# Giving the decoding of w_out its own tiles and a later turn, and re-running the order search of a fused attention and gated-MLP kernel

## The chip, the cores and the metric

One core of a Trainium2 chip runs the whole program. The metric is the device time of one execution in microseconds (us). The kernel before takes 417.23 us (median of 3 runs, 416.99 to 417.38). PE is the matmul engine, PEld its weight loads, DVE the vector engine, ACT the scalar engine, POOL the GpSimd engine, and SP the engine that issues every DMA here.

## The reference

The inputs are four batches of 768 positions with 8 heads of 64. Everything is in f32 except that some weights come as f64, which the kernel must decode itself.

```
scores = (q @ k^T) / 8;  keep key j for query i if j < 4 or 0 <= i - j < 128
a      = softmax(scores over the kept keys);   x = a @ v           (heads side by side: 512 columns)
h      = relu(x @ w_in)  (512 -> 1024);        u, v = halves of h
vn     = (v - mean(v)) / sqrt(var(v) + 1e-6)   (over the 512 columns)
vs     = w_spatial @ vn + b_spatial            (mixes the 768 positions of a batch)
out    = (u * vs) @ w_out                      (512 -> 512)
```

## The kernel before

Positions are cut into tiles of 128, so a batch has six. A tile's attention is done in two halves of four heads; the 48 halves of the four batches are numbered 0 to 47. The program speaks of *pieces*, each a few instructions of one engine:

- **Attention.** SP loads `qkraw` and `vraw`. PE makes scores (`sc`), DVE adds the mask and finds the row's extreme (`pexp` and `nm`, L1022), ACT takes the exponential (L1027). The weights are split into a high and a low f16 part (`p`; a helper's lines, L698 or L707 for the high part, L714 for the low). SP turns both with DMA transposes (`pT`), PE multiplies with the values (`av`), DVE divides (`x`, L1132 to L1134). The same split and transposing give `xT`.
- **MLP.** PE makes `ps_v` and `ps_u` from `xT` and w_in. ACT applies the relu (`vr`, `u`), DVE and POOL normalise `vr` and split it into `vn`. When all six tiles of a batch have their `vn`, PE makes the twelve *spatial products* `ps_s` of that batch. DVE gates them (`g`, L1243, then L1247 on DVE or POOL), they are split into `g2`, and PE makes the six *output products* `ps_o`. ACT copies them out (`ob`), SP stores them.
- **Precision.** Nearly every product is three f16 matmuls (high by high, high by low, low by high). Twelve matmuls make one piece `ps_v`, `ps_u` or `ps_o`, 18 make one `ps_s`.
- **Decoding.** w_in (eight chunks of 128 by 512) and w_out (four chunks) come as f64 bit patterns. Each chunk is loaded by SP (`dec`, 512 KB), goes through two steps of ACT (L793 into `w32`, L795 into `wtmp`), three of DVE (L791, L798, L800, on `w32`), an add on POOL (L803), a high part on ACT (L700) and a low part on DVE (L721). Listings show `w32` as `w`, often with a number.
- **Checks.** Maxima of all tables are gathered. At the very end of the program PE, DVE and PE again turn them into one flag (`allmax`, `ps_row`, `ps_col`, `marks`, `found`, L762 to L898). All engines read the flag and branch.

**What sets the order.** Nothing is scheduled by the hardware beyond each engine's own queue, which runs in program order. A planner in the kernel (`Plan`) sorts the pieces by rank (the table `WHEN`, in units of one attention half), derives what must follow what, and then plays all pieces through a model of the engines; whoever may start first in that model goes next, and may also choose the engine of a piece that has several (`ENGINES`). `order()` then repeats: it plays the result backwards to get every piece's distance to the end, shakes these distances by a random amount per kind or per piece, and plays forward again. The list `PASSES` holds the seeds, the sizes of the shaking and the numbers of repetitions. Its last result is the program.

Tiles come from rings of places. `"u"` (seven places), for one, is shared by `u`, the raw w_spatial rows and `dec`; `"vn"` (twelve) by `vn` and `w32`; `"vr"` (three) by `vr`, `ob` and `wtmp`. In the rings that `IN_TURN` lists, `"u"` and `"vn"` among them, a tile gets its place strictly in the order of the ranks. PSUM for the MLP products is a ring of two banks (`"mm"`), so each product waits until the product before the last has been read out by ACT or DVE.

Of the kernel before, what the change touches and what calls it, by code (L numbers as in the profile page):

```python
# [70 lines left out]
def general_path(tc, wf, qk, v, w_in, w_sp, b_sp, w_out, out):  # L71
# [164 lines left out]
UB, VNB, G2B, XTB, P16B, PTB, QKB, QPB, PEB, VB, VRB = 7, 12, 12, 2, 2, 2, 2, 2, 2, 3, 6  # L236
GB = 2

WHEN = {
# [3 lines left out]
    "u gap": 1.24, "u relu": 0.2, "s": 2.69, "s gap": 0.68, "s rest": 0.0, "gate": 0.0, "g split": 0.41, "o": 0.2,  # L243
    "o gap": 0.0, "o copy": 0.36, "o store": 0.44, "w_in 1": -5.48, "w_in 0": -0.25, "w_sp": 5.67, "w_out": 3.53,
    "w_in 1 gap": 0.0, "w_in 0 gap": 0.75, "w_sp gap": 0.24, "w_out gap": 1.39,
}
# [79 lines left out]
class Plan:  # L326
# [183 lines left out]
    def order(self):  # L510

        self.prepare()
        kinds, kind = {}, {}
        for p in self.pieces:
            name, which = ((p[6] or p[5])[0])[:2]
            key = name, str(which[0] if isinstance(which, tuple) else which), p[2] if isinstance(p[2], str) else ""
            kind[p[1]] = kinds.setdefault(key, len(kinds))
        self.end = self.settle([p[0] for p in self.ps])
        for seed, of_kind, of_piece, passes in PASSES:
            for k in range(passes):  # L520
                prio = self.backward()
                if k == 0:
                    prio = [x + of_kind / 100.0 * scatter(seed, kind[p[1]]) + of_piece / 100.0 * scatter(seed + 7936, 100000 + p[1])
                            for x, p in zip(prio, self.ps)]
# [68 lines left out]
def fast_path(tc, st, scalars, qk, v, v0, vs, w_in, w_sp, w_rows, b_sp, b_col, w_out, out):  # L593
# [7 lines left out]
    with (  # L601
# [40 lines left out]
        def next_p16(name):  # L642
# [6 lines left out]
            "w32": ("vn", sb([P, 512], F32, "vn", VNB)), "vn": ("vn", sb([P, 2, DM], F16, "vn", VNB)),  # L649
            "wtmp": ("vr", sb([P, 512], I32, "vr", VB)), "vr": ("vr", sb([P, DM], F32, "vr", VB)),  # L650
            "ob": ("vr", sb([P, DM], F32, "vr", VB)),
# [18 lines left out]
                 "p16": P16B, "pT": PTB, "x": 1, "x16": 2, "xT": XTB, "g": GB, "g2": G2B,  # L670
                 "sc": BANKS["sc"], "av": BANKS["av"], "mm": BANKS["mm"], "ksink": 1}
        rings.update({f"{kind}{j}": 1 for kind in ("kslot", "vslot", "vsink") for j in range(4)})
# [110 lines left out]
        def decode(rank, src, i, c, f0):  # L783

            words = lambda: tl("dec", i).rearrange("p (n two) -> p n two", two=2)
            lo, hi = lambda: words()[:, :, 0], lambda: words()[:, :, 1]
            w = lambda: tl("w32", i)
# [17 lines left out]

# [39 lines left out]
        def w_out_all():  # L845
            r0, gap = WHEN["w_out"], WHEN["w_out gap"]
            for c in range(KC):
                i = ("out", 0, c)
                decode(r0 + gap * c, w_out, i, c, 0)
                high(r0 + gap * c, "w_in high", 512, lambda c=c, i=i: (wout[:, 0, c, :], tl("w32", i)),  # L850
                     [("w32", i)], [("wout", c, 0)], OUT_SCALE)
                low_scaled(r0 + gap * c, 512, lambda c=c, i=i: (wout[:, 1, c, :], tl("w32", i), wout[:, 0, c, :]), OUT_SCALE,
                           [("w32", i), ("wout", c, 0)], [("wout", c, 1)])
# [98 lines left out]
        def whole(b):  # L952
            return b < WHOLE
# [35 lines left out]
        def scores(i, b, t, hf, h2, r, n):  # L989
# [35 lines left out]
            def exped(q):  # L1025
# [3 lines left out]
            keys = [(f"kslot{kslot(b, x)}", (b, x)) for x in ((t, t - 1, 5) if t == 4 else (t, t - 1) if t else (t,))]  # L1029
            plan.add(r, "PE", (0.06 + n / 4 * (1.04 if t else 0.56)) if whole(b) else 0.03 + n / 2 * (0.336 if t else 0.18), product,  # L1030
                     ([("qkraw", (b, t)), ("k0room", 0)] if whole(b) else [("qp", (b, t))]) + keys, banks,
# [176 lines left out]
        def u_half(b, c0, d, r):  # L1208
# [3 lines left out]
            def product(e):  # L1212
# [8 lines left out]
            k = first["u"] + (b * NT // 2 + c0) * KC + d  # L1221
            plan.add(r + WHEN["u relu"], "a", 0.55, lambda e: nc.scalar.activation(  # L1222
                tl("u", (b, c0))[:, d, :], tl("ps_u", i)[:, :TC], AF.Relu, scale=G_SCALE / (V_SCALE * IN_SCALE),
# [155 lines left out]
```

## Time and profile before

| | us |
|---|---|
| median of 3 runs (416.99 to 417.38) | 417.23 |
| the profiled execution, its own time | 416.92 |
| its span, first to last instruction | 415.1 |
| PE busy (share of the span) | 389.8 (94%) |
| DVE busy | 325.7 (78%) |
| ACT busy | 299.3 (72%) |
| POOL busy | 164.9 (40%) |
| chain that ended last: PE / DVE / ACT | 63% / 26% / 4% |

A busy share is a mean over the whole span, and this program has two halves that differ, so the share of each stretch is read and not the mean. The chain that ended last is followed back from the last instruction: each piece in it is what released the next one.

### The profile page before, as it was taken

Reading aid. Unit: us, or ns where it says so; the run is one execution under the profiler, and the core shown is the slowest. Engines: PE = TensorE matmul, PEld = TensorE weight load, DVE = VectorE, ACT = ScalarE, POOL = GpSimd, SP = SyncE. Lnnn points to the kernel's source line nnn. Section 1 sums busy time; section 2 is a strip of 40 time slices with the busy share of each in tenths; the row PEclk is TensorE's granted clock in tenths of the full one; section 3 lists DMA queues with packets and bytes.
Section 4 is the critical chain, followed back from the end, with each engine's and each line's share of the span. In section 5 each row is a group of like instructions: output and inputs, shape, how many; then the busy total and the mean of one; then the engine's idle time right before and its main releaser. Section 6 shows DMA issues by size and latency. Waiting matters only on the chain.

```text
span 415.1 us, 9851 instructions
## 1 busy us (share of the span) xinstructions
PE 389.8 (94%) x3635; PEld 274.7 (66%) x3635; DVE 325.7 (78%) x908; ACT 299.3 (72%) x695; POOL 164.9 (40%) x204
## 2 busy tenths in 40 slices
PE   3899699899999999999999999999999999999992
PEld 2686355667766757667767677577677686688740
DVE  2999999999999989878899797787897855256311
ACT  4987989888897788687867886858567643366740
POOL 4442345763755645324454853233236432100000
PEclk9999998999999999999999999999999999999998
DMA  7999999978478788757968587594783493602011
GB/s 229 386 325 252 267 202 181 222 115 172 108 168 173 187 152 198 182 120 148 221 159 182 81 208 183 130 209 93 148 173 89 86 201 34 204 27 76 37 66 58
DMA packets 137047, 66.93 MB, mean 161 GB/s; under 512 B 118432, under 2 KB 122272, under 8 KB 136992
## 3 DMA queue, kind: packets, MB, share of 16 engines
q1 hardware_dynamic: 136992, 66.24, 70.3%
q8 instruction: 30, 0.49, 0.5%
q14 instruction: 25, 0.20, 0.2%
HBM read 31.09 MB, written 6.29 MB: 90 GB/s over the span
## 4 chain that ended last, share of the span: by engine, by line
PE 63%; DVE 26%; ACT 4%; issue 3%; DMA 3%; SPq 0%; DVEq 0%; ACTq 0%
PE ps_s L732 19%; PE ps_o L732 14%; PE ps_u L732 11%; PE ps_v L732 9%; DVE pexp L1022 5%; DVE p L714 5%; PE sc L1017 5%; ACT pexp L1027 2%; PE av L1112 2%; DMA dec<-w_in 2%; PE av L1113 2%; PE av L1114 2%; DVE vring L721 1%; DVE w L791 1%; DVE wsp L721 1%
## 5 line engine op out<-in xcount | busy, mean ns | idle before, releaser
L1027 ACT ACTIVATE pexp<-pexp,nm 128x260 f32<-128x260 f32 (+1 forms) x192 | 82.9, 484 | 24.9 <-DVE nm L1022 24.5
L732 PE MATMUL ps_s<-wsp,vn 128*128 128x256 f16 x864 | 99.3, 273 | 0.8 <-DVE g L1243 0.4
L732 PEld LDWEIGHTS <-vn 128*128 128x128 f16 x864 | 83.5, 98 | 14.4 <-issue 3.1
L732 PE MATMUL ps_v<-win,xT 128*128 128x512 f16 x288 | 69.1, 391 | 3.6 <-DMA xT<-x 3.2
L732 PE MATMUL ps_u<-xT,win 128*128 128x256 f16 x576 | 69.7, 275 | 2.8 <-ACT vr L1173 1.9
L732 PE MATMUL ps_o<-wout,g 128*128 128x512 f16 x288 | 65.3, 379 | 1.2 <-DVE g L1243 0.4
L732 PEld LDWEIGHTS <-win 128*128 128x128 f16 x576 | 55.2, 98 | 13.9 <-issue 5.3
L714 DVE TENSOR_TENSOR p<-pexp,p 128x16 f16<-128x16 f32 (+2 forms) x65 | 50.0, 783 | 7.5 <-ACT p L698 6.3
L732 PEld LDWEIGHTS <-xT 128*128 128x128 f16 x288 | 27.8, 100 | 36.7 <-issue 5.7
L732 PEld LDWEIGHTS <-g 128*128 128x128 f16 x288 | 27.5, 98 | 32.6 <-issue 2.2
L714 POOL TENSOR_TENSOR x<-x,x 128x512 f16<-128x512 f32 x24 | 30.9, 1290 | 38.3 <-ACT x L698 36.6
L698 ACT CAST p<-pexp 128x1024 f16<-128x1024 f32 (+2 forms) x68 | 40.6, 621 | 1.3 <-DMA pT<-p 0.7
L1243 DVE SCALAR_TENSOR_TENSOR g<-ps_s,b_bc 128x256 f32<-128x256 f32 x48 | 20.2, 422 | 19.1 <-PE ps_s L732 18.6
L1112 PE MATMUL av<-vring,pT 128*128 128x65 f16 x328 | 34.1, 193 | 0.0
L1114 PE MATMUL av<-vring,pT 128*128 128x65 f16 x328 | 34.0, 193 | 0.0
L1113 PE MATMUL av<-vring,pT 128*128 128x65 f16 x328 | 34.0, 193 | 0.0
L1112 PEld LDWEIGHTS <-pT 128*128 128x128 f16 x328 | 30.2, 97 | 1.5 <-issue 0.6
L1189 POOL TENSOR_TENSOR rs<-rs,mhalf 128x1 f32<-128x1 f32 x24 | 16.3, 681 | 36.9 <-DVE rs L1183 31.5
L1113 PEld LDWEIGHTS <-pT 128*128 128x128 f16 x328 | 30.1, 97 | 0.6
L1222 ACT ACTIVATE u<-ps_u 128x256 f32<-128x256 f32 x48 | 18.2, 379 | 16.6 <-PE ps_u L732 16.4
L1114 PEld LDWEIGHTS <-pT 128*128 128x128 f16 x328 | 30.0, 97 | 0.0
L698 ACT CAST g<-g 128x256 f16<-128x256 f32 x36 | 14.5, 403 | 20.4 <-DVE g L1247 18.2
(139 smaller groups left out, 722.4 us busy)
## 6 DMA issues: line engine op xcount, KB each, us to landing
qkraw<-qk_t SPq DMA_DIRECT2D x18, 512.0 KB, 4.4
out<-ob SPq DMA_DIRECT2D x24, 256.0 KB, 2.5
vraw<-v_s SPq DMA_DIRECT2D x22, 256.0 KB, 3.7
dec<-w_in SPq DMA_DIRECT2D x8, 512.0 KB, 8.4
wrow<-w_sp_rows SPq DMA_DIRECT2D x6, 384.0 KB, 4.8
dec<-w_out SPq DMA_DIRECT2D x4, 512.0 KB, 6.5
wsp<-qk_t SPq DMA_DIRECT2D x6, 256.0 KB, 6.7
qkraw<-qk_t SPq DMA_DIRECT2D x6, 256.0 KB, 5.1
```

The source lines that it names most:

```text
L698: nc.scalar.copy(o, x)
L714: eng[e].tensor_tensor(out=o, in0=x, in1=hi, op=ALU.subtract)
L732: nc.tensor.matmul(o, a, m, start=(i == 0), stop=(i == n - 1))
L1017: nc.tensor.matmul(o, qp[rows, qi, hp, :], keys(kring[:, ki], rows), start=(m == 0), stop=(m == 2))
L1022: nc.vector.tensor_tensor_reduce(out=po, in0=o, in1=mask, scale=-0.125 if whole(b) else -0.125 / Q_SCALE ** 2, scalar=3.0e38, op0=ALU.add, ...
L1027: nc.scalar.activation(po, po, AF.Exp, bias=nm()[:, h2 + q:h2 + q + 1], scale=-1.0)
L1112: nc.tensor.matmul(o[:, h], ph, vh, start=(t < 2 and j == 0), stop=False)
L1113: nc.tensor.matmul(o[:, h], ph, vl, start=False, stop=False)
L1114: nc.tensor.matmul(o[:, h], pl, vh, start=False, stop=(j == nb - 1 and (t < 2 or h == HH - 1)))
L1189: nc.gpsimd.tensor_tensor(out=vals["rs", i], in0=vals["rs", i], in1=mhalf, op=ALU.pow)
L1222: plan.add(r + WHEN["u relu"], "a", 0.55, lambda e: nc.scalar.activation(tl("u", (b, c0))[:, d, :], tl("ps_u", i)[:, :TC], AF.Relu, scale= ...
L1243: nc.vector.scalar_tensor_tensor(out=g(), in0=tl("ps_s", i)[:, :TC], scalar=1.0 / (SP_SCALE * VNS), in1=b_bc[:, t0:t0 + TC], op0=ALU.mult, ...
```

## The change

Three things are edited. First, the four chunks of w_out get tiles of their own: `dec2`, `w32b` and `wtmp2`, each a ring of one place, instead of places in the rings `"u"`, `"vn"` and `"vr"`. Second, the rank of w_out goes from 3.53 to 12.0 (behind the twelve halves of batch 0), its gap from 1.39 to 0.5. Third, the order search: `PASSES` is replaced, two planning costs are altered (scores after batch 0, and the relu of `u`), and a pass may now have zero repetitions. Such a pass does not play backwards; it shakes the distances in use, and with `near` only those around one point of time. No instruction is added or removed; some move to another engine, and most stand elsewhere.

```diff
+WB = 1
-    ... "w_sp": 5.67, "w_out": 3.53,
-    "w_in 1 gap": 0.0, "w_in 0 gap": 0.75, "w_sp gap": 0.24, "w_out gap": 1.39,
+    ... "w_sp": 5.67, "w_out": 12.0,
+    "w_in 1 gap": 0.0, "w_in 0 gap": 0.75, "w_sp gap": 0.24, "w_out gap": 0.5,
-PASSES = ((411092411, 231, 0, 2), (411092412, 34, 0, 1), ...
+PASSES = ((384001216, 948, 203, 5), (384001217, 765, 315, 4), ..., (388001173, 72, 0, 0), ...
+def near(seed, x):
+    if seed >> 6 & 1:
+        return 1.0
+    u = (mix(seed, 7) + 1) / 2
+    return 1.0 if abs(x - u * u * 430.0) < 5.0 + 20.0 * (mix(seed, 8) + 1) else 0.0
...
+        prio = [p[0] for p in self.ps]
         for seed, of_kind, of_piece, passes in PASSES:
-            for k in range(passes):
-                prio = self.backward()
+            for k in range(max(passes, 1)):
+                if passes:
+                    prio = self.backward()
                 if k == 0:
-                    prio = [x + of_kind / 100.0 * scatter(...) + of_piece / 100.0 * scatter(...)
+                    prio = [x + near(seed, x) * (of_kind / 100.0 * scatter(...) + of_piece / 100.0 * scatter(...))
                             for x, p in zip(prio, self.ps)]
                 self.end = self.settle(prio)
...
+            "dec2": ("dec2", sb([P, 1024], I32, "dec2", 1)), "w32b": ("w32b", sb([P, 512], F32, "w32b", WB)), "wtmp2": ("wtmp2", sb([P, 512], I32, "wtmp2", 1)),
...
         def decode(rank, src, i, c, f0):
+            dec, w32, wtmp = ("dec2", "w32b", "wtmp2") if i[0] == "out" else ("dec", "w32", "wtmp")
...
-            plan.add(r, "PE", ... else 0.03 + n / 2 * (0.336 if t else 0.18), product,
+            plan.add(r, "PE", ... else 0.14 + n / 2 * (0.325 if t else 0.17), product,
...
-            plan.add(r + WHEN["u relu"], "a", 0.55, ...
+            plan.add(r + WHEN["u relu"], "a", 0.37, ...
```

**Where it moves instructions.** The first place is the queue of SP early in the program. Before, from the load of the first w_spatial chunk on:

```order
L830 DMA wsp<-w_sp_t 128x768
L726 DMA dec<-w_out 128x1024
L1152 DMA_TRANSPOSE xT<-x_379 128x8x128
L726 DMA dec<-w_out 128x1024
L1074 DMA_TRANSPOSE pT<-p_0_135 128x8x128
L1074 DMA_TRANSPOSE pT<-p_0_135 128x9x128
L726 DMA vraw<-v_s 128x512
L830 DMA wsp<-w_sp_t 128x768
```

Now, from the load of the third w_spatial chunk to the same transposes:

```order
L843 DMA wsp<-w_sp_t 128x768
L738 DMA dec_402<-w_out 128x1024
L1165 DMA_TRANSPOSE xT<-x_371 128x8x128
L738 DMA vraw<-v_s 128x512
L843 DMA b_bc<-w_sp_t 128x768
L1087 DMA_TRANSPOSE pT<-p_0_135 128x8x128
L1087 DMA_TRANSPOSE pT<-p_0_135 128x9x128
L843 DMA wraw<-w_sp_t 128x768
```

Of the four loads of w_out, three stood ahead of the fifth pair of `pT` transposes before, and the fourth soon behind; now only the first stands there. The loads of w_spatial have gone forward into their room. The other three stand where the attention of batch 1 is under way:

```order
L738 DMA qkraw<-qk_t 128x2x512
L738 DMA dec_1613<-w_out 128x1024
L1165 DMA_TRANSPOSE xT<-x_1637 128x8x128
L738 DMA vraw<-v_s 128x512
L738 DMA qkraw<-qk_t 128x2x512
L738 DMA vsraw<-v_sink 96x260
L1087 DMA_TRANSPOSE pT<-p_0_135 128x8x128
L738 DMA dec_1761<-w_out 128x1024
```

These are the third and the fourth; each new load can go only when the DVE step that reads the one `dec2` place has ended.

The second place is the queue of DVE just ahead of the first spatial product, which needs the `vn` of all six tiles of batch 0. Before (`w_1384` is the last chunk of w_out; the other three had their three DVE steps long before):

```order
L791 TENSOR_SCALAR w_1384<-w_1384 128x512
L721 SCALAR_TENSOR_TENSOR wsp<-wraw,wsp 128x768
L1197 TENSOR_SCALAR vr<-vr,mv,rs 128x512 x2
L721 SCALAR_TENSOR_TENSOR wsp<-b_bc,wsp 128x768
L714 TENSOR_TENSOR vn<-vr,vn 128x512 x2
L1132 TENSOR_SCALAR den<-av 128x8
L1133 RECIPROCAL den<-den 128x8
L1134 TENSOR_TENSOR x<-av,den 128x512
L798 TENSOR_SCALAR w_1384<-w_1384 128x512
```

Now (the first chunk of w_out had its three steps shortly before; `w32b` is the one place):

```order
L726 TENSOR_TENSOR vn<-vr,vn 128x512
L1210 TENSOR_SCALAR vr<-vr,mv,rs 128x512
L733 SCALAR_TENSOR_TENSOR wsp<-wraw,wsp 128x768
L726 TENSOR_TENSOR vn<-vr,vn 128x512
L1145 TENSOR_SCALAR den<-av 128x8
L1146 RECIPROCAL den<-den 128x8
L1147 TENSOR_TENSOR x<-av,den 128x512
L733 SCALAR_TENSOR_TENSOR vring<-vraw,vring 128x8x64
L733 SCALAR_TENSOR_TENSOR wout<-w32b,wout 128x512
L733 SCALAR_TENSOR_TENSOR kring<-qkraw,kring 128x4x128
L804 TENSOR_SCALAR w32b<-w32b 128x512
L1256 SCALAR_TENSOR_TENSOR g<-ps_s,b_bc 128x256
```

The second, third and fourth chunk are now decoded between the spatial products of batch 0, one after the other.

The third place is the end of the queue of DVE. Before:

```order
L714 TENSOR_TENSOR g_6314<-g,g_6314 128x256
L878 TENSOR_REDUCE most<-sums 128x4
L769 TENSOR_REDUCE allmax_6343<-ps_row 1x1
L776 COPY allmax_r<-ps_col 128x1
L881 TENSOR_REDUCE most<-sums 128x4
L882 TENSOR_SCALAR most<-most,allmax_r 128x4
L883 TENSOR_SCALAR marks<-most 128x13
L884 TENSOR_SCALAR marks<-most 128x13
L892 TENSOR_SCALAR found<-ps_row 1x13
```

Now:

```order
L781 TENSOR_REDUCE allmax_6272<-ps_row 1x1
L788 COPY allmax_r<-ps_col 128x1
L894 TENSOR_REDUCE most<-sums 128x4
L895 TENSOR_SCALAR most<-most,allmax_r 128x4
L896 TENSOR_SCALAR marks<-most 128x13
L897 TENSOR_SCALAR marks<-most 128x13
L1256 SCALAR_TENSOR_TENSOR g<-ps_s,b_bc 128x256
L1260 TENSOR_TENSOR g<-g,u 128x256
L726 TENSOR_TENSOR g_6329<-g,g_6329 128x256
L905 TENSOR_SCALAR found<-ps_row 1x13
```

The `marks` of the checks now stand ahead of the last two gates; only the count on PE and the `found` steps are left behind the last output product.

## Rows read from the trace of the kernel before

**Rows 1.** Busy us of each engine in a stretch of 10 us (columns as in Rows 2).
```profile
60.00:70.00 10.00, 8.25 (x88) 5.85 (x87) 9.83 (x28) 9.98 (x24) 4.04 (x5) 0.83 0.90 201
```

**Rows 2.** The same view, cut where PE's work changes.
```profile
core 0: us, PE busy (x) PEld busy (x) DVE busy (x) ACT busy (x) POOL busy (x), PEclk, DMA share, GB/s
0.00:105.38 105.38, 89.92 (x728) 62.56 (x729) 95.64 (x263) 87.23 (x196) 51.65 (x79) 0.97 0.98 234
105.38:146.77 41.39, 39.77 (x382) 28.78 (x381) 41.06 (x104) 34.33 (x78) 23.37 (x25) 1.00 0.73 157
146.77:406.93 260.16, 259.79 (x2525) 183.29 (x2524) 187.47 (x534) 177.11 (x423) 89.87 (x101) 1.00 0.61 136
406.93:415.10 8.17, 0.28 (x2) 0.10 (x2) 1.50 (x11) 0.60 (x1) 0.00 (x0) 0.79 0.12 42
```

**Rows 3.** The chain that ended last: start, us, what.
```profile
144.27 1.13 DVE p L714
146.77 2.75 PE ps_o L732 x12
149.52 0.77 PE sc L1017 x12
150.51 0.03 PE av L1112
...
185.34 2.59 PE ps_v L732 x12
```

**Rows 4.** PE in order of time, behind the first spatial products; idle in brackets.
```profile
112.74 2.13 PE L732 MATMUL ps_s<-wsp,vn 128*128 128x256 f16 x18 [0.42 <-DVE g L1243]
```

**Rows 5.** Groups of DVE in 0 to 105.38 us: count, busy us, mean ns.
```profile
L714 DVE TENSOR_TENSOR p<-pexp,p 128x1024 f16<-128x1024 f32 x9 | 12.1, 1340 | 0.5 <-ACT p L698 0.3
L800 DVE SCALAR_TENSOR_TENSOR w<-dec,w 128x512 int32<-128x512 int32 x11 | 7.5, 683 | 0.1
L791 DVE TENSOR_SCALAR w<-w 128x512 f32<-128x512 f32 x12 | 7.4, 617 | 2.2 <-ACT w L793 2.2
L798 DVE TENSOR_SCALAR w<-w 128x512 int32<-128x512 int32 x11 | 6.0, 545 | 0.0
...
L721 DVE SCALAR_TENSOR_TENSOR vring<-vraw,vring 128x512 f16<-128x512 f32 x6 | 5.3, 884 | 0.0
...
L1134 DVE TENSOR_TENSOR x<-av,den 128x512 f32<-128x512 f32 x7 | 4.8, 692 | 0.4
...
L721 DVE SCALAR_TENSOR_TENSOR qp<-qkraw,qp 128x512 f16<-128x512 f32 x3 | 3.1, 1041 | 0.0
L714 DVE TENSOR_TENSOR vn<-vr,vn 128x512 f16<-128x512 f32 x4 | 2.6, 684 | 0.0
L721 DVE SCALAR_TENSOR_TENSOR kring<-qkraw,kring 128x512 f16<-128x512 f32 x3 | 2.0, 683 | 0.0
```

**Rows 6.** DVE in order of time ahead of the first spatial product: start, us.
```profile
103.94 1.29 DVE L714 TENSOR_TENSOR vn<-vr,vn 128x512 f16<-128x512 f32 x2
```

**Rows 7.** The same view of the whole span: the narrow low part.
```profile
L714 DVE TENSOR_TENSOR p<-pexp,p 128x512 f16<-128x512 f32 x3 | 2.1, 688 | 1.5 <-ACT p L698 1.5
```

**Rows 8.** PE in order of time at the end.
```profile
401.59 5.34 PE L732 MATMUL ps_o<-wout,g 128*128 128x512 f16 x24 [0.37 <-DVE allmax L769]
406.86 0.17 PE L772 MATMUL ps_col<-allmax,ones 1*128 1x1 bf16 x1
407.94 0.17 PE L887 MATMUL ps_row<-marks,ones 128*1 128x26 bf16 x1 [0.91 <-DVE marks L884]
```

**Rows 9.** DMA issues of 15 to 60 us: KB, median us to landing.
```profile
dec<-w_out SPq DMA_DIRECT2D x4, 512.0 KB, 6.5
...
pT<-p SPq DMA_TRANSPOSE x9, 4.8
```

**Rows 10.** DMA issues of 90 to 125 us.
```profile
qkraw<-qk_t SPq DMA_DIRECT2D x3, 512.0 KB, 4.2
...
pT<-p SPq DMA_TRANSPOSE x8, 3.9
```

**Rows 11.** DMA issues of the whole span (the page).
```profile
dec<-w_in SPq DMA_DIRECT2D x8, 512.0 KB, 8.4
```

More of the change, by code (lines that the diff above doesn't have):

```diff
@@ L243 @@
     "u gap": 1.24, "u relu": 0.2, "s": 2.69, "s gap": 0.68, "s rest": 0.0, "gate": 0.0, "g split": 0.41, "o": 0.2,
-    "o gap": 0.0, "o copy": 0.36, "o store": 0.44, "w_in 1": -5.48, "w_in 0": -0.25, "w_sp": 5.67, "w_out": 3.53,
-    "w_in 1 gap": 0.0, "w_in 0 gap": 0.75, "w_sp gap": 0.24, "w_out gap": 1.39,
+    "o gap": 0.0, "o copy": 0.36, "o store": 0.44, "w_in 1": -5.48, "w_in 0": -0.25, "w_sp": 5.67, "w_out": 12.0,
+    "w_in 1 gap": 0.0, "w_in 0 gap": 0.75, "w_sp gap": 0.24, "w_out gap": 0.5,
 }
@@ L649, in fast_path @@
             "w32": ("vn", sb([P, 512], F32, "vn", VNB)), "vn": ("vn", sb([P, 2, DM], F16, "vn", VNB)),
-            "wtmp": ("vr", sb([P, 512], I32, "vr", VB)), "vr": ("vr", sb([P, DM], F32, "vr", VB)),
+            "wtmp": ("vr", sb([P, 512], I32, "vr", VB)),
+            "dec2": ("dec2", sb([P, 1024], I32, "dec2", 1)), "w32b": ("w32b", sb([P, 512], F32, "w32b", WB)), "wtmp2": ("wtmp2", sb([P, 512], I32, "wtmp2", 1)), "vr": ("vr", sb([P, DM], F32, "vr", VB)),
             "ob": ("vr", sb([P, DM], F32, "vr", VB)),
@@ L670, in fast_path @@
                  "p16": P16B, "pT": PTB, "x": 1, "x16": 2, "xT": XTB, "g": GB, "g2": G2B,
-                 "sc": BANKS["sc"], "av": BANKS["av"], "mm": BANKS["mm"], "ksink": 1}
+                 "dec2": 1, "w32b": WB, "wtmp2": 1, "sc": BANKS["sc"], "av": BANKS["av"], "mm": BANKS["mm"], "ksink": 1}
         rings.update({f"{kind}{j}": 1 for kind in ("kslot", "vslot", "vsink") for j in range(4)})
@@ L783, in decode @@
         def decode(rank, src, i, c, f0):
-            words = lambda: tl("dec", i).rearrange("p (n two) -> p n two", two=2)
+            dec, w32, wtmp = ("dec2", "w32b", "wtmp2") if i[0] == "out" else ("dec", "w32", "wtmp")
+            words = lambda: tl(dec, i).rearrange("p (n two) -> p n two", two=2)
             lo, hi = lambda: words()[:, :, 0], lambda: words()[:, :, 1]
-            w = lambda: tl("w32", i)
+            w = lambda: tl(w32, i)
             ci = lambda: w().bitcast(I32)
@@ L849, in w_out_all @@
                 decode(r0 + gap * c, w_out, i, c, 0)
[L850 to L853, printed above, removed]
+                high(r0 + gap * c, "w_in high", 512, lambda c=c, i=i: (wout[:, 0, c, :], tl("w32b", i)),
+                     [("w32b", i)], [("wout", c, 0)], OUT_SCALE)
+                low_scaled(r0 + gap * c, 512, lambda c=c, i=i: (wout[:, 1, c, :], tl("w32b", i), wout[:, 0, c, :]), OUT_SCALE,
+                           [("w32b", i), ("wout", c, 0)], [("wout", c, 1)])
             for k in range(2):
@@ L1029, in scores @@
             keys = [(f"kslot{kslot(b, x)}", (b, x)) for x in ((t, t - 1, 5) if t == 4 else (t, t - 1) if t else (t,))]
-            plan.add(r, "PE", (0.06 + n / 4 * (1.04 if t else 0.56)) if whole(b) else 0.03 + n / 2 * (0.336 if t else 0.18), product,
+            plan.add(r, "PE", (0.06 + n / 4 * (1.04 if t else 0.56)) if whole(b) else 0.14 + n / 2 * (0.325 if t else 0.17), product,
                      ([("qkraw", (b, t)), ("k0room", 0)] if whole(b) else [("qp", (b, t))]) + keys, banks,
@@ L1221, in u_half @@
             k = first["u"] + (b * NT // 2 + c0) * KC + d
-            plan.add(r + WHEN["u relu"], "a", 0.55, lambda e: nc.scalar.activation(
+            plan.add(r + WHEN["u relu"], "a", 0.37, lambda e: nc.scalar.activation(
                 tl("u", (b, c0))[:, d, :], tl("ps_u", i)[:, :TC], AF.Relu, scale=G_SCALE / (V_SCALE * IN_SCALE),
```

18 lines of the change are left out of this document (9 added, 9 removed).

## Prediction

> **What bounds the kernel now.** I read the busy times by stretch first, since the shares over the whole span mix two halves [rows 2]. Ahead of the first spatial product (0 to 105.38 us) DVE is busy for 95.64 of 105.38, PE for 89.92. From there to 146.77 DVE has 41.06 of 41.39 and PE 39.77, so PE stands still for 1.62. From 146.77 to 406.93 PE has 259.79 of 260.16: 0.37 of idle time in 260. So DVE sets the pace up to about 146 and PE behind it. The chain that ended last says the same: it is on DVE until `p` at 144.27, and from 146.77 on PE follows PE [rows 3]. The last 8.17 us are the checks, the flag and the branches, with almost nothing busy [rows 2].
>
> The time of the end is therefore a sum: when the first spatial product can start (it needs everything that DVE does for batch 0), the PE work that then remains, PE's idle time behind it, and the tail. Before, this is 105.38, then 406.93 - 105.38 = 301.55, of which 1.62 + 0.37 = 1.99 is idle time and 299.56 work, then 8.17 [rows 2]. A microsecond that DVE saves ahead of 105 is worth something only if PE does not lose it again, and a piece of PE that stood ahead of the first spatial product and now stands behind it costs its full length.
>
> **DVE ahead of the first spatial product.** By the orders of before and after, 167 pieces of DVE stand ahead of it before and 157 after. The difference, each count by the mean of its group [rows 5, 7]:
> - Decoding of w_out: before ten of its twelve DVE steps stand there (the order's second place shows the last of them), now three. Three clamps fewer at 0.617, two at 0.545 and two at 0.683: -4.31.
> - Low parts of `p` that POOL did and DVE does now: one of 128x1024 at 1.340 and two of 128x512 at 0.688: +2.72.
> - Two low parts of `vn` at 0.684, which go to POOL or behind: -1.37. One `kring` (0.683), one `qp` (1.041), one `vring` (0.884) and one `x` (0.692), which now come later: -3.30.
>
> Together -6.26. Neighbours on DVE overlap a little: the pair of `vn` takes 1.29 for two [rows 6], where two at 0.684 are 1.37, so 0.08 a piece, and 0.8 for ten. I take **-5.5**: the first spatial product at 99.9 instead of 105.38. The bounds: no overlap and the DVE waits for ACT's decode steps gone for three of twelve chunks (2.2 x 3/12 = 0.55) gives -6.9; three new waits of a low `p` for ACT, at the 1.5 of three in [rows 7], give -4.0.
>
> **PE ahead and behind.** Four PE pieces that stood ahead of the first spatial product now stand behind it: one `sc` (0.77), one `ps_v` (2.59) and two `av` of 24 matmuls at 0.03 (0.72 each) [rows 3]. That is **+4.8**, to 304.36. It eats most of the first term, and I see no range in it: the pieces are counted, and PE was at full granted clock there (1.00) [rows 2].
>
> **PE's idle time behind it.** The decode of three chunks (7 steps), and the other pieces, now lie among the spatial products of batch 0, where DVE had 0.33 us free in 41.39. They are covered only by the 4.8 of PE work that stands there now too. Before, two of the five waits of this stretch are for DVE's `g`, 0.42 each (one of them is [rows 4]). Counted piece by piece with the group means, DVE's work up to what each later product needs, plus PE's work behind that product, grew by 0.5 over the stretch before; after, it falls by up to 1.2. So I take those two waits as gone, **-0.85**. Bounds: all of 1.99 gone but 0.4, or nothing gone.
>
> **The tail.** Before, the last output product ends at 406.93, and the count of the marks comes at 407.94, after 0.91 of waiting for DVE's `marks` [rows 8]. After, `marks` is made ahead of the last two gates (the order's third place), so the count can follow the last output product at once: -0.9. In return `ps_row`, `allmax` and `ps_col` (0.17) [rows 8] stand amid PE's last work; the wait for `allmax` there was 0.37 already, and I add 0.15 for `ps_col` and a dearer wait. **-0.7** (bounds -0.9 and -0.4).
>
> **Loads and the single place.** The three later chunks share one `dec2`, one `w32b` and one `wtmp2`, so the load of the next is issued only when DVE has read the place of the last: load, two ACT steps and DVE's clamp stand in one line. DVE and ACT work in order; if a load is late, ACT waits at L793's successor with `u`, `vr` and `ob` queued behind it, and PE with its two `mm` banks soon waits for those. By the order 6 to 7.5 us of DVE work lie between the issue of a load and the clamp that needs it. A 512 KB load landed in 4.2 us in 90 to 125 us [rows 10], 6.5 in 15 to 60 [rows 9], 8.4 for w_in [rows 11]. The stage is that of 90 to 125, so I take the first of these and no wait. That is the cost priced at nothing, with its cover; without it, 8.4 - 4.2 = 4.2.
>
> **Sum.** -5.5 + 4.8 - 0.85 - 0.7 = -2.25, on the profiled execution's own 416.92: 414.7. The median of the runs lies 0.31 above that execution, so the forecast is **415.0**. All bounds on one side give -6.9 + 4.8 - 1.6 - 0.9 = -4.6, on the other -4.0 + 4.8 + 0 - 0.4 = +0.4; they will not all fall together, and I take 413.2 to 416.6 as the forecast's own range.
>
> **The rivals.**
> 1. *Slower: the line of w_out loads holds DVE and ACT.* For it: one place instead of many, DMA shares of 0.98 up to 105 [rows 2], and a load that took 6.5 and 8.4 elsewhere [rows 9, 11]. Against: the DMA share falls to 0.73 behind 105 [rows 2]. It decides when a load needs more than some 6 us from issue. At 8.4 one clamp is late by about 2, and three chunks in line by 4.2 to 6 in all; with 4.2 over the forecast it is 415.0 + 4.2 = 419.2. Small lateness (6.5 us, three times 0.5) gives 416.5 and lies in the forecast.
> 2. *No change: the transposes pay.* Three loads of 512 KB now stand in SP's queue among the `pT` transposes of batch 1 (the order's first place). A `pT` landed in 4.8 us where w_out was loaded before [rows 9] and in 3.9 where it was not [rows 10]. If PE gets 0.9 less three times, with nothing in stock, that is 2.7, and the time 417.6. For it: SP is the only issuing engine. Against: PE waited for no transpose of that stage by the trace. A variant with the same result: ACT, 9.98 of 10 in 60 to 70 us [rows 1], is the joint bound ahead of the first spatial product, so that DVE's 5.5 arrives as half.
> The Trainium skill speaks for this rival: "DMA: Bandwidth & Descriptors", section "Queues, rings and completion order", says that on each DMA engine descriptors are consumed in ring order, so a transpose issued behind a 512 KB load would start behind it; the 4.8 against 3.9 agrees in sign. By the rule taken fully, each of the three `pT` would come later by the whole 4.2 us of a load, and the time would be worse than this rival's; the trace's 0.9 bears out a fifth of that, and the chance below rests on the 0.9.
> 3. *More gain: the granted clock.* In 60 to 70 us the granted clock is 0.83, PE busy 8.25 [rows 1]; it dips after PE's idle stretches, and fewer loads now stand ahead of the first `xT` transposes, so PE may stand still less. For 105 us PE idles for 15.46 [rows 2]. PE is not the bound there, so this pays only through earlier `ps_v` and `vr`, hence earlier DVE; if a third of DVE's 9.74 idle (105.38 - 95.64) goes, the time is 415.0 - 3.2 = 411.8.
>
> **How the numbers follow.** Forecast 0.54, rival 1 0.18, rival 2 0.17, rival 3 0.11. A measurement of this kernel can tell about 0.2% (0.8 us) from no change. The forecast's own range reaches to 416.6, and a tenth of its chance lies inside the 0.8: faster is 0.49 + 0.11 + a share of rival 2 of 0.02 = 0.62, no change 0.05 + 0.13 = 0.18, slower 0.18 + 0.02 = 0.20. The range leaves out half of rival 1 and half of rival 3 and a little else: 411.9 to 418.6.
>
> **What would show it.** The first `ps_s` should start near 99.9 (105.38 before), with 157 pieces of DVE ahead of it; one `sc`, one `ps_v` and two `av` should come later than it; PE's idle time from there to the last `ps_o` should be near 1.1; the count of the marks should stand directly behind the last `ps_o`, and the span end some 7.4 us after that product. The forecast is wrong if DVE's or ACT's first decode steps of w_out wait for the load (rival 1), if PE's waits for `av` on `pT` grow in 100 to 145 us (rival 2), if the first `ps_s` comes at 97 or earlier (rival 3), or if it comes at 99.9 and PE idles behind it for 4 us or more.

## The result, and the profile after

The changed kernel takes 411.58 us (median of 3 runs, 410.94 to 411.74) against 417.23: a ratio of 0.9857, 95% interval 0.9838 to 0.9877. It is 5.65 us faster, where 2.2 were forecast, and 0.3 below the low end of the range (411.9). Its profiled execution spans 409.1 us against 415.1.

The same cut by stretches as in [rows 2], at the changed kernel's own first spatial product (95.57) and last output product (402.24):

```profile
core 0: us, PE busy (x) PEld busy (x) DVE busy (x) ACT busy (x) POOL busy (x), PEclk, DMA share, GB/s
0.00:95.57 95.57, 82.66 (x657) 57.57 (x657) 86.24 (x247) 81.89 (x183) 43.69 (x74) 0.91 0.92 230
95.57:145.00 49.43, 48.33 (x514) 35.33 (x512) 48.89 (x122) 46.02 (x107) 29.95 (x30) 1.00 0.86 210
145.00:402.24 257.24, 256.57 (x2470) 180.07 (x2467) 187.63 (x526) 173.35 (x409) 86.80 (x106) 1.00 0.62 133
402.24:409.10 6.86, 0.11 (x2) 0.01 (x1) 0.75 (x6) 0.60 (x1) 0.00 (x0) 0.80 0.14 50
```

The prediction's sum, term by term (before from [rows 2]):

| us | before | after | forecast | measured |
|---|---|---|---|---|
| first spatial product starts | 105.38 | 95.57 | -5.5 | -9.8 |
| PE work from there to the last output product | 299.56 | 304.90 | +4.8 | +5.3 |
| PE idle in the same stretch | 1.99 | 1.10 + 0.67 = 1.77 | -0.85 | -0.2 |
| tail | 8.17 | 6.86 | -0.7 | -1.3 |
| sum | 415.1 | 409.1 | -2.25 | -6.0 |

So it is the first term that was wrong, by 4.3; the others are within 0.7. Before and after are one profiled execution each.

PE in order of time there (start, duration, idle before it):

```profile
95.57 2.37 PE L744 MATMUL ps_s<-wsp,vn 128*128 128x256 f16 x18
98.64 0.19 PE L1125 MATMUL av<-vring,pT 128*128 128x65 f16 x1 [0.70 <-DVE x L1147]
99.15 0.19 PE L1126 MATMUL av<-vring,pT 128*128 128x65 f16 x1 [0.32 <-DVE vring L733]
```

and DVE at the same time:

```profile
94.84 0.68 DVE L726 TENSOR_TENSOR vn<-vr,vn 128x512 f16<-128x512 f32 x1
95.44 0.54 DVE L1210 TENSOR_SCALAR vr<-vr,mv,rs 128x512 f32<-128x512 f32 x1
95.90 0.95 DVE L733 SCALAR_TENSOR_TENSOR wsp<-wraw,wsp 128x768 f16<-128x768 f32 x1
96.77 0.68 DVE L726 TENSOR_TENSOR vn<-vr,vn 128x512 f16<-128x512 f32 x1
```

The last `vn` of batch 0 ends at 97.45, against 105.23 before (103.94 + 1.29, [rows 6]): -7.8. And the first product no longer begins behind it: its 18 matmuls wait one by one, and by the trace's start times all but the last three begin by 97.33, while DVE is still at work on the last tile. Before, the start stood 0.15 behind the last `vn`, now 1.88 ahead of it. The two make the -9.8.

DVE's groups up to the last `vn` (0 to 97.45 us; count, busy, mean ns), beside [rows 5] and [rows 7]:

```profile
L726 DVE TENSOR_TENSOR p<-pexp,p 128x1024 f16<-128x1024 f32 x10 | 13.5, 1354 | 0.0
L813 DVE SCALAR_TENSOR_TENSOR w<-dec,w 128x512 int32<-128x512 int32 x8 | 7.2, 923 | 0.1
L804 DVE TENSOR_SCALAR w<-w 128x512 f32<-128x512 f32 x8 | 4.3, 534 | 2.6 <-ACT w L806 2.6
L811 DVE TENSOR_SCALAR w<-w 128x512 int32<-128x512 int32 x8 | 3.3, 422 | 0.1
L726 DVE TENSOR_TENSOR p<-pexp,p 128x512 f16<-128x512 f32 x2 | 2.2, 1103 | 0.0
L733 DVE SCALAR_TENSOR_TENSOR qp<-qkraw,qp 128x512 f16<-128x512 f32 x2 | 1.4, 684 | 0.0
L804 DVE TENSOR_SCALAR w32b<-w32b 128x512 f32<-128x512 f32 x1 | 0.4, 421 | 0.0
```

The same instruction has different means in the two kernels: the clamp (L791, now L804) 617 before, 534 and 421 now; `qp` 1041 before, 684 now. Others rose: `w<-dec,w` from 683 to 923, the narrow low part of `p` from 688 to 1103. Before's own trace shows why. DVE and then POOL at 33 us:

```profile
32.74 0.69 DVE L721 SCALAR_TENSOR_TENSOR win<-w,win 128x512 f16<-128x512 f32 x1
33.34 1.77 DVE L721 SCALAR_TENSOR_TENSOR vring<-vraw,vring 128x512 f16<-128x512 f32 x1
35.03 1.49 DVE L798 TENSOR_SCALAR w<-w 128x512 int32<-128x512 int32 x1
36.55 0.69 DVE L800 SCALAR_TENSOR_TENSOR w<-dec,w 128x512 int32<-128x512 int32 x1
```

```profile
33.17 3.06 POOL L803 TENSOR_TENSOR w<-w,wtmp 128x512 int32<-128x512 int32 x2 [6.79 <-ACT wtmp L795]
```

POOL's two adds run from 33.17 to 34.56 and from 34.70 to 36.23. The DVE step at 33.34 takes 1.77 where its neighbours of the same size take 0.69, and the one at 35.03 takes 1.49 where the same step elsewhere takes 0.41 (74.28, shown at the end): each began while one of the adds ran, and ended 0.55 and 0.29 behind it. I call this *standing under POOL*. To sum it, I subtract from each DVE instruction's duration the value that the fastest tenth of its form stays below: up to the start of the first spatial product and 2 us beyond it this is 14.3 us before and 11.2 after. Of that, 12.8 before and 9.8 after lie in DVE steps (24 and 18 of them, each over by more than 0.1) that ended behind a POOL step that had run beside them. That this sum would change by 3 us was not looked for in the prediction.

Of the steps that were priced at nothing, the single place held. The three later loads landed in time, one of them narrowly: by the trace's times of landing the load issued at 103.83 landed at 108.88, and ACT's first step on it began at 108.96.

```profile
dec<-w_out SPq DMA_DIRECT2D x3, 512.0 KB, 4.0
...
pT<-p SPq DMA_TRANSPOSE x7, 3.2
```

(90 to 125 us.) No DVE or ACT step waited for them, and `pT` landed in 3.2 us beside them, sooner than the 3.9 of [rows 10]. No `pT` was issued while one of these loads was on its way, though (the nearest stands at 119.60, behind the load of 113.81 that landed at 117.72), so what such a load costs a `pT` directly behind it is not shown here. Rivals 1 and 2 did not happen. Nor did rival 3 as it was put: the granted clock ahead of the first product is lower than before (0.91 against 0.97), and DVE's idle time there is 95.57 - 86.24 = 9.33 us, where 9.74 was to fall by a third. The time came out beside rival 3's 411.8, and the first `ps_s` ahead of its mark of 97, but by luck: its mechanism is not in the trace.

The tail, PE in order of time (`ps_col` is now at 390.22):

```profile
390.22 0.16 PE L784 MATMUL ps_col<-allmax,ones 1*128 1x1 bf16 x1 [0.37 <-DVE allmax L781]
...
402.17 0.17 PE L900 MATMUL ps_row<-marks,ones 128*1 128x26 bf16 x1
```

The 0.91 of waiting for `marks` in [rows 8] is gone, as forecast.

### The profile page after: what moved, and what is told of

Same layout as the page of the kernel before. It is cut to its first block, busy times and chain, and to the rows that moved or that the text cites. A ratio compares the mean times of both kernels' runs of the same rounds, so it can differ in the third digit from the quotient of the medians.

```text
span 409.1 us, 9861 instructions
## 1 busy us (share of the span) xinstructions
PE 387.7 (95%) x3635; PEld 273.0 (67%) x3635; DVE 323.5 (79%) x899; ACT 301.9 (74%) x699; POOL 160.4 (39%) x209
## 4 chain that ended last, share of the span: by engine, by line
PE 73%; DVE 15%; issue 6%; DMA 2%; POOL 2%; ACT 1%; SPq 1%; DVEq 0%; POOLq 0%; ACTq 0%
PE ps_s L744 22%; PE ps_o L744 15%; PE ps_v L744 12%; PE ps_u L744 11%; PE sc L1030 5%; DVE pexp L1035 3%; DVE p L726 2%; PE av L1125 2%; PE av L1126 2%; PE av L1127 2%; DMA dec<-w_in 1%; DVE vr L1210 1%; DVE w L813 1%; PE sc L1024 1%; DVE st L1192 1%
## 5 line engine op out<-in xcount | busy, mean ns | idle before, releaser
L1040 ACT ACTIVATE pexp<-pexp,nm 128x260 f32<-128x260 f32 (+1 forms) x192 | 81.5, 483 | 16.4 <-DVE nm L1035 16.0
L744 PE MATMUL ps_u<-xT,win 128*128 128x256 f16 x576 | 67.9, 273 | 2.1 <-DMA xT<-x 0.9
L726 DVE TENSOR_TENSOR p<-pexp,p 128x1024 f16<-128x1024 f32 (+2 forms) x72 | 61.7, 867 | 2.6 <-ACT p L710 2.3
L710 ACT CAST p<-pexp 128x32 f16<-128x32 f32 (+2 forms) x71 | 43.3, 639 | 0.8
L1030 PE MATMUL sc<-kring,qp 64*128 64x260 f16 (+1 forms) x432 | 29.0, 263 | 0.5 <-DVE qp L733 0.3
```

The source lines that it names most:

```text
L710: nc.scalar.copy(o, x)
L726: eng[e].tensor_tensor(out=o, in0=x, in1=hi, op=ALU.subtract)
L744: nc.tensor.matmul(o, a, m, start=(i == 0), stop=(i == n - 1))
L1030: nc.tensor.matmul(o, qp[rows, qi, hp, :], keys(kring[:, ki], rows), start=(m == 0), stop=(m == 2))
L1040: nc.scalar.activation(po, po, AF.Exp, bias=nm()[:, h2 + q:h2 + q + 1], scale=-1.0)
```

## The experiments

Three theories stood against each other at first: that the decoding's places and turn make the gain, by freeing DVE ahead of the first spatial product, that it comes from the order search, or that it comes from the loads being gone from the early queue. Each run is compared by its ratio to the kernel before on the same chip. The changed kernel itself, run twice more beside them (c0_after, e0_after), gave 0.9841 [0.9809, 0.9874] and 0.9851 [0.9832, 0.9871]: some 0.985, to which the others are held.

> The changed kernel itself, once more, so that its variants stand beside it on one chip. 0.984 to 0.988 of the kernel before, by all theories.

> The changed kernel once more, for the comparison: 0.984 to 0.987 of the kernel before, by all theories.

The last `vn` of batch 0 ends at 97.39 and 98.00 in these two, and at 97.45 in the trace above. Executions of one order differ early: the same `w<-dec,w` step of DVE begins at 13.01 in c0_after, 13.22 in the trace above, 14.66 in d1_pool_wide and 15.21 in b1_dve_ahead, ahead of the first of the subtractions that these last two add. So a last `vn` from one trace is good to 1 or 2 us, and the ends are compared by medians.

**The parts one by one.** Places and turn with the old seeds and costs (`PASSES`, `near` and the two costs as before):

> The changed kernel with the old seeds and the old planning costs: only the places of w_out's tiles and their turn are new, and the order is found again from the old seeds. If places and turn make the gain (decoding out of the way ahead of the first spatial product): 411 to 414 us. If the search makes it: 416 us or more, since the old seeds were found for another set of pieces; then DVE's work ahead of the first spatial product is shorter by the seven decoding steps (about 3 us) and PE's idle time does not fall with it.

Measured 1.0047 [1.0026, 1.0069]: slower than before. The run does not test the later turn, though: in its trace ten DVE steps on w_out's tiles (eight on `w32b`, two on `wout`) stand ahead of the first product, as many as before, where the changed kernel has three. The last `vn` comes at 105.21. The new search with the old places and turn (`"w_out": 3.53`, gap 1.39, `dec`, `w32`, `wtmp`):

> The changed kernel with w_out decoded in the shared places and at its old turn: only seeds, small steps and planning costs are new. If the search makes the gain: 411 to 414 us. If places and turn make it: 416 us or more. If both are needed together, this one and the one with the old search are both at 416 or more.

Measured 1.0285 [1.0254, 1.0317]. Neither half has any of the gain. The seeds were found for one set of pieces, and with another they give another order, so the split by parts can't be had this way. In a2_search the last `vn` comes only at 120.84, and PE waits 12.2 us in all for `nm`. Without the small steps (only the 15 passes with repetitions):

> The changed kernel without the 105 passes of zero repetitions (the small steps); the 15 ordinary passes stay. If the small steps at the end carry part of the gain: 413 to 415.5 us, and the checks at the end or PE's short waits are worse. If places, turn and ordinary passes are enough: 411 to 412.4 us.

Measured 0.9868 [0.9831, 0.9904]; the small steps bring between nothing and some 0.5%, which these runs don't tell apart.

**The tail alone,** on the kernel before, its order kept:

```
+ for x in (col, r, marks): order.remove(x)
+ k = at(("1", "gate")) + 1            # behind the maximum of ps_row
+ order[k:k] = [col, r, marks]
```

> The kernel before, its order kept, but ps_col, its copy and the marks of the checks moved up to where ps_row stands, ahead of the last two output products. Theory: the count then follows the last output product at once, -0.9 us, and the wait for allmax and ps_col amid PE's work costs 0.2 to 0.5: together -0.4 to -0.8, that is 416.4 to 416.8 us. Rival (the flag and the branches behind the count take what they take and the saving is lost in them): no change, 417.2.

Measured 0.9982 [0.9965, 1.0000], -0.75 us, with an interval that just reaches no change. PE in order of time:

```profile
402.32 0.16 PE L781 MATMUL ps_col<-allmax,ones 1*128 1x1 bf16 x1 [0.37 <-DVE allmax L778]
402.48 5.34 PE L741 MATMUL ps_o<-wout,g 128*128 128x512 f16 x24
407.75 0.17 PE L896 MATMUL ps_row<-marks,ones 128*1 128x26 bf16 x1
```

The count follows the product directly. The forecast's 0.7 for the tail agrees; the 1.3 of the one profiled execution has in it 0.2 of the way behind the count (7.16 against 6.93 us) and the 0.17 of `ps_col`, which now stands amid PE's work.

**What DVE's time is worth, ahead and behind.** On the changed kernel, order kept, five extra steps that write a spare tile:

```
+ nc.vector.tensor_tensor(out=spare[:, 1], in0=spare[:, 0], in1=spare[:, 0], op=ALU.subtract)   # x5
```

> The changed kernel, its order kept, with five extra DVE steps of 128x512 f32 (about 0.6 us each, 3.0 together; they only write a spare tile) among the last 15 DVE pieces ahead of the last vn of batch 0. Theory (what DVE has to do up to that vn bounds the end): the last vn moves from 97.45 to about 100.5, and the end by +2.3 to +3.0 us. Rival (PE's own work is the bound by now, DVE has slack there): less than +0.8.

Measured 0.9932 [0.9908, 0.9957]: about 0.8%, 3.4 us over the changed kernel, for 3.0 us of DVE. What is done ahead costs its full length, with some 1.3 us of uncertainty. This run also shows what the first product's lead over the last `vn` is worth, since here it has none:

```profile
102.40 2.13 PE L744 MATMUL ps_s<-wsp,vn 128*128 128x256 f16 x18
104.37 0.19 PE L1125 MATMUL av<-vring,pT 128*128 128x65 f16 x1
```

```profile
101.46 0.68 DVE L726 TENSOR_TENSOR vn<-vr,vn 128x512 f16<-128x512 f32 x1
```

Against the changed kernel's trace the last `vn` comes 4.7 later (2.0 of it there at the `w<-dec,w` step named above, before the added steps), the first product 6.8 later, and the span is 5.0 longer. So of the 2.1 us of lead that are lost 0.3 are seen at the end: the two `av` behind the product no longer wait, and PE's idle time from the product on is 0.52 instead of 1.77.

> The same five extra DVE steps, put among the DVE pieces of 102 to 120 us, behind the first spatial product of batch 0, where the decoding of w_out now stands. Theory (DVE hands the bound to PE at the last vn, about 97 us): +0 to +1.2 us, and less than half of what the same steps cost ahead of it. Rival (DVE is the bound up to some 145 us, as the chain of the kernel before had it): +2.3 to +3.0, as much as ahead.

Measured 0.9909 [0.9886, 0.9933]: about 2.5 us over. PE's stretch behind the first product, and its waits from there on:

```profile
95.94:145.00 49.06, 44.59 (x437) 31.89 (x435) 48.54 (x114) 42.41 (x99) 29.35 (x29) 1.00 0.76 190
```

```profile
PE ps_v L744 <- DVE g L1256: 2.7, 2, 1.7
PE ps_u L744 <- DVE g L1256: 0.7, 2, 0.4
```

PE idles 4.47 there instead of 1.10, for DVE's `g`. So DVE bounds on to about 145 in the changed kernel too, and my theory that it hands over at the last `vn` falls. By the two runs, carrying 3 us of DVE from ahead to behind is worth about 0.9 us, with an uncertainty of 1.4. As far as that goes, the later turn of w_out by itself is a small part of the 5.65.

**The loads.** Three more loads at the old places in SP's queue:

```
+ nc.sync.dma_start(spare, w_out.bitcast(I32)[k * P:(k + 1) * P, :1024])   # about 17, 28, 46 us
```

> The changed kernel, its order kept, with three more loads of 512 KB from w_out into a spare tile, at the places in SP's queue where the kernel before had three of its w_out loads (about 17, 28 and 46 us). Nothing reads them. Rival theory (the gain comes from SP's queue and the DMA engines being rid of these loads early, so that xT, pT and qkraw arrive sooner): +1.5 to +3 us, with PE's wait for xT near 48 us longer by 1 or more. Theory of DVE: less than +0.6.

Measured 0.9868 [0.9829, 0.9907], 0.8 us over 0.985 and not told apart from it. PE's wait for `xT` is 1.9 us, where the changed kernel without them has 2.0, so the rival's own sign is missing. Its price is not excluded, since the interval reaches 2.4 us over 0.985. In the trace the last `vn` comes at 99.99, 2.5 later than 97.45; 1.1 of this is there at the same early `w<-dec,w` step (14.31 against 13.22), and most of the rest is one clamp that now falls under an add of POOL:

```profile
28.68 1.48 DVE L804 TENSOR_SCALAR w<-w 128x512 f32<-128x512 f32 x1
```

```profile
28.50 1.37 POOL L816 TENSOR_TENSOR w<-w,wtmp 128x512 int32<-128x512 int32 x1 [0.90 <-ACT wtmp L808]
```

**Standing under POOL.** On the kernel before, the twelve adds cut to 128x8:

```
- out=ci(), in0=ci(), in1=tl("wtmp", i), op=ALU.add)
+ out=ci()[:, :8], in0=ci()[:, :8], in1=tl("wtmp", i)[:, :8], op=ALU.add)
```

> The kernel before, its order kept, with POOL's twelve adds of the decoding cut from 128x512 to 128x8 (so the low bits of the decoded weights are left out). In its trace about 4 us of DVE's time ahead of the first spatial product is DVE steps that took up to twice as long while one of these adds ran. Theory (such collisions are part of what DVE has to do, and the bound): DVE's steps there get shorter by 3 to 4.5 us together, and the end comes 2 to 4 us earlier. Rival (PE stood without a gap from 82 to 105 us, so DVE's earlier end is lost): 0 to -0.8.

Measured 0.9866 [0.9844, 0.9888]: -5.6 us, as much as the whole change, and more than expected. DVE's groups in 0 to 105.2 us of this run (its first product starts at 102.20), beside [rows 5]:

```profile
L714 DVE TENSOR_TENSOR p<-pexp,p 128x1024 f16<-128x1024 f32 x9 | 11.2, 1242 | 0.5 <-ACT p L698 0.3
L791 DVE TENSOR_SCALAR w<-w 128x512 f32<-128x512 f32 x12 | 5.9, 492 | 2.3 <-ACT w L793 2.2
L798 DVE TENSOR_SCALAR w<-w 128x512 int32<-128x512 int32 x12 | 5.0, 418 | 0.0
```

L798 falls from 545 to 418, L791 from 617 to 492, with nothing in them changed; the sum of standing falls from 14.3 to 8.3. In the trace the last `vn` comes 3.2 earlier (102.04 against 105.23); the rest of the gain lies behind that. But decoding also ends some 1.2 us sooner per chunk in this run, so I split the adds in four instead of cutting them:

> The kernel before, its order kept, with the same twelve adds as four of 128x128 each. It tells what made the gain of the run with adds of 128x8 on this kernel (-5.6 us). Theory (DVE's waits under the adds): -2.5 to -4.5 us here as well. Rival (there the decoding of each chunk ended about 1.2 us sooner, and that made it): 0 or slower, since each chunk's add now takes longer.

Measured 0.9961 [0.9943, 0.9979], -1.6 us, less than the theory wanted; standing falls to 11.6, DVE's last `vn` comes only 0.3 earlier. That this is because each chunk takes longer is not shown. The two effects stay mixed here. On the changed kernel:

> The changed kernel, its order kept, with each of POOL's twelve adds of the decoding (128x512, 1.27 us undisturbed) as four of 128x128. Theory (a DVE step that starts under a POOL step stands until that POOL step ends, so shorter POOL steps cost DVE less): DVE's steps ahead of the first spatial product get shorter by 1.5 to 3 us together, and the end comes 1 to 2.5 us earlier, in spite of the adds taking longer themselves. Rival (the two slow each other in proportion to the time they run together): no gain, 0 to +1 us, since the four take longer than the one.

Measured 0.9829 [0.9802, 0.9855] beside 0.9841 of the changed kernel on the same chip: no difference that can be told, where the theory wanted 1 to 2.5 us; standing 10.4 instead of 11.2. With all wide POOL subtractions split:

> The changed kernel, its order kept, with all of POOL's wide subtractions (low parts of x, vn, p) in four pieces as well as the adds. Theory of DVE standing under a POOL step: a further 1 to 2 us beyond the run with the adds alone, that is 407 to 410 us. Rival: POOL's own time grows by some 0.8 us for each of about 60 steps, and PE waits for xT and vn: 413 or more.

Measured 1.0007 [0.9988, 1.0027]: the rival. Standing falls to 8.8, but POOL's steps take longer and PE idles 4.8 us behind the first product.

The clean test adds POOL steps that nobody waits for, where POOL is idle:

```
+ nc.gpsimd.tensor_tensor(out=spare[:, 1, :w], in0=spare[:, 0, :w], in1=spare[:, 0, :w], op=ALU.subtract)   # x6, w = 512 or 8
```

> The changed kernel, its order kept, with six extra POOL subtractions of 128x512 f32 (about 1.2 us each) on a spare tile, where POOL is idle for 1.5 us or more and that nobody waits for (behind 28, 45, 56, 61, 72 and 92 us). Theory (a DVE step that starts under a POOL step stands until it ends): DVE's steps up to the last vn of batch 0 get longer by 2.5 to 5 us together, the last vn comes that much later, and the end by +2 to +5 us. Rival (POOL beside DVE costs nothing by itself; the change's gain is in the order alone): less than +0.8.

> The same six POOL steps at the same places, of 128x8 (about 0.28 us each). Theory: DVE stands under them for 0 to 0.2 us each; together less than +0.8 at the end. If the number of extra POOL instructions and not their length made the cost of the wide ones, this one costs as much.

Measured 0.9890 [0.9870, 0.9910] for the wide ones and 0.9849 [0.9827, 0.9870] for the narrow ones on the same chip: 0.4%, 1.7 us, between them, a little under what was expected. One of them, DVE and then POOL of the run with wide steps:

```profile
30.05 0.45 DVE L811 TENSOR_SCALAR w<-w 128x512 int32<-128x512 int32 x1
30.42 0.42 DVE L1035 CUSTOM_DVE_ANT_0 pexp<-sc,m_even 128x260 f32<-128x260 f32 x1
30.77 0.91 DVE L811 TENSOR_SCALAR w<-w 128x512 int32<-128x512 int32 x1
31.60 0.68 DVE L813 SCALAR_TENSOR_TENSOR w<-dec,w 128x512 int32<-128x512 int32 x1
```

```profile
30.18 1.22 POOL L1336 TENSOR_TENSOR spare<-spare 128x512 f32<-128x512 f32 x1
```

POOL's spare step ends at 31.40, the DVE step under it at 31.68, 0.28 later, with a length of 0.91 instead of 0.42: it stood until POOL was done, and then ran. The `pexp` at 30.42 ran beside the same POOL step in its usual 0.42. Four of the six steps caught a DVE step, by 0.50, 0.77, 0.85 and 0.50, together 2.6 us. The last `vn` of the wide run and that of the narrow run:

```profile
100.83 0.68 DVE L726 TENSOR_TENSOR vn<-vr,vn 128x512 f16<-128x512 f32 x1
```

```profile
98.06 0.68 DVE L726 TENSOR_TENSOR vn<-vr,vn 128x512 f16<-128x512 f32 x1
```

The wide run's comes 2.8 later, of which 0.8 was there at the early `w<-dec,w` step (14.66 against 13.90), so some 2.0 are the wide steps' doing. POOL's own work was not held up by them: behind each of the six its next step still waited, for 0.19 us or more, on another engine or a load. With no work and no dependency added to DVE, its standing alone moves the end.

The Trainium skill has this rule on the page "SBUF — State Buffer", section "Who interferes with whom": VectorE and GpSimd share a pair of ports, which is an exclusive lock, held for the whole instruction; the loser is blocked, not slowed. The 0.28 after POOL's end agrees with blocking, and the `pexp` with its statement that only some VectorE instructions take the pair. In the prediction it would have spoken for counting those collisions.

**Can the planner use it?** It weighs such an overlap with 0.7. With 0.95 behind the last pass, and 714 further small steps kept from a search:

> The changed kernel with another order: behind its last pass the planner counts 0.95 instead of 0.7 of the time for which DVE and POOL would use the shared way together, and goes on with 714 small steps kept from a search. Theory (DVE's standing under POOL ahead of the first spatial product is part of the bound): less of it in the trace (below 9 us instead of 11.2), last vn earlier, and the end at 0.978 to 0.983 of the kernel before, that is 408.5 to 410.8 us. Rival (the planner's other errors, waits for DMA and PE's clock above all, are larger than this one): 0.984 to 0.990, no better than the changed kernel.

Measured 0.9835 [0.9809, 0.9862] beside 0.9851 on the same chip. Standing fell to 8.5, as the theory wanted, but the last `vn` stayed at 97.75 and the time did not move. So less standing is not by itself an earlier `vn` in another order. The outcome is the rival's; which other errors of the planner outweigh it is not shown. No version was found that is clearly faster than the changed kernel.

## Why the prediction was wrong

- **The bound.** Right: DVE up to about 145, PE behind it. The runs with five extra DVE steps show it in the changed kernel for both sides of the first product.
- **DVE ahead of the first spatial product: the step that failed.** The count was right (250 DVE instructions up to the last `vn` instead of 262, as by the list), but -5.5 should have been -7.8 for the last `vn`. I took the durations of the DVE steps that stay as fixed by the kernel before, and they are not. The group means of [rows 5] hold standing under POOL: a clamp costs 0.42 undisturbed, not 0.617, and `qp` 0.68, not 1.041. With undisturbed durations the same list gives about -5.0 instead of -6.26, so some 1.3 of standing was in my figure without my knowing. Measured, standing fell by some 3.0. The missing 1.7 and a first DVE step that came 0.6 earlier (5.52 instead of 6.11) are the 2.3 by which the term was short. The condition was in the trace before: the means of L791 (617) and L798 (545) both lie well above the 0.41 that the step takes when nothing disturbs it.
- **How far this is shown.** That such standing moves the end is shown by the wide and narrow POOL steps. That it makes the 3 us of this change rests on the trace alone, and a fall of standing need not arrive: it fell by 6.0 in b5_noadd for 3.2 at the last `vn`, by 2.7 in c2_before_split for 0.3, and by 2.7 in d3_port for nothing. The -7.8 itself is a difference of two traces; with 105.97 in a4_tail, whose order up to there is that of before, and 97.39 to 98.00 in the changed kernel it is 7.2 to 8.6.
- **The start of the product at the last `vn`.** I took a product to need all six tiles at its start. It starts 1.88 us ahead of the last one, where it started 0.15 behind it: this is the other 2.0 of the 4.3 by which the term was off. Of a lead of this size hardly anything is seen at the end, by b1_dve_ahead, where it was lost and 0.3 of its 2.1 us were; the changed kernel gives it back in the waits of the two `av`.
- **PE ahead and behind.** +4.8 was +5.3: `sc`, `ps_v` and the two `av` came behind, as forecast, and the first product has 0.24 of waiting inside it (2.37 against 2.13 in [rows 4]).
- **PE's idle time.** The two waits for `g` went, as forecast, but the two `av` now wait 0.70 and 0.32 for DVE, which I had not seen, and the product's lead is what exposes them: -0.2 instead of -0.85.
- **The tail.** Right in mechanism, since the wait for `marks` is gone in both traces; -0.75 (0 to -1.5) by the run that moved it alone.
- **The range.** Its low end took in rival 3 by half and no case in which DVE's durations themselves change, so it ended 0.3 too high. Two slips in the working change nothing: the low bound of the DVE term is -6.26 - 0.55 = -6.8, not -6.9, and rival 2's time 417.7, not 417.6.

## What to carry to other kernels

A mean duration is not the price of an instruction where two engines hold each other up: it holds the waiting of the order in which it was measured. Price a removed step at its undisturbed duration, and count separately how often the new order lets any step start under the other engine's; the first without the second would have been further off here than the means were (-5.0 against -6.26, for -7.8). Where an order search is part of a change, its parts can't be undone one by one; keep the order and add or take away time at one place instead. A group of matmuls that reads several producers' tiles can start before the last of them is done (1.88 us here), and such a lead is worth something only if PE does not wait directly behind it.

## What was not expected

- Cutting twelve POOL steps from 1.45 us mean to 0.28 on the kernel before was worth 5.6 us, with PE the engine that is 94% busy.
- PE ran at a mean granted clock of 0.91 ahead of the first product in the changed kernel (0.97 before) and had that product 9.8 us earlier. The mean hides two levels: 0.50, that is 1.2 GHz, from 27.4 to 41.1 and from 47.9 to 51.3 us, which began in or right behind idle stretches of PE of 1.3 and 2.0 us, and 1.00, that is 2.4 GHz, elsewhere. In e0_after, the same kernel, it was 0.98:

```profile
0.00:95.57 95.57, 80.43 (x651) 56.65 (x652) 85.38 (x246) 81.82 (x183) 43.34 (x74) 0.98 0.94 229
```

  Its DVE was 0.9 later at the early `w<-dec,w` step (14.10 against 13.22) and its last `vn` 0.55 later (98.00), so the lower clock of the first trace cost 0.3 us at most that can be seen.
- POOL stands for DVE as well, it seems. In d1_pool_wide the same spare step of POOL took 1.04 us at 76.11 and 2.02 at 95.99, where a `p` of DVE ran until 97.11:

```profile
94.83 2.29 DVE L726 TENSOR_TENSOR p<-pexp,p 128x1024 f16<-128x1024 f32 x1
```

```profile
76.11 1.04 POOL L1336 TENSOR_TENSOR spare<-spare 128x512 f32<-128x512 f32 x1
95.99 2.02 POOL L1336 TENSOR_TENSOR spare<-spare 128x512 f32<-128x512 f32 x1
```

  At 70 us of the kernel before both directions seem to follow on each other: two `p` of DVE take 4.04 together, where an undisturbed one takes 1.21, and a `p` of POOL 2.23. The undisturbed clamp is the last DVE line here:

```profile
70.32 4.04 DVE L714 TENSOR_TENSOR p<-pexp,p 128x1024 f16<-128x1024 f32 x2
74.28 0.41 DVE L798 TENSOR_SCALAR w<-w 128x512 int32<-128x512 int32 x1
```

```profile
70.07 1.26 POOL L803 TENSOR_TENSOR w<-w,wtmp 128x512 int32<-128x512 int32 x1
72.10 2.23 POOL L714 TENSOR_TENSOR p<-pexp,p 128x1024 f16<-128x1024 f32 x1 [0.77 <-ACT p L698]
```
